# Residual rows added by accumulating DMAs in the second MLP product

## The chip, the cores and the metric

The kernel runs on one core of one Trainium2 chip. A core has TensorE (matrix products, PE in the profile), VectorE (DVE), ScalarE (ACT), GpSimd (POOL) and SyncE (SP), each with a queue of its own that is worked off in order, and 16 DMA engines that move data between HBM, which all queues share, and the core's own memory SBUF. TensorE writes its results to PSUM, in banks of 128 x 512 float32. The metric is the device time of one execution in microseconds, lower is better; of several runs the median is given.

## What is computed

A transformer block on a sequence of 2048 tokens with 1024 channels, in float32: attention with a compressive memory, then an MLP with 3584 hidden channels, each with a residual connection. What matters here is the last part:

```python
h = x + attention(layernorm(x))
y = layernorm(layernorm(h))
h2 = h + gelu(y @ w1 + b1) @ w2 + b2
```

The change concerns the last line: the product of the hidden activations with `w2` (2048 x 3584 times 3584 x 1024), and how `h + b2` is added to it.

## The kernel before

**Precision.** A float32 product is made of three faster ones: both operands are split into a high and a low part (`h`, `l`), and high x high, high x low and low x high are added up in a PSUM bank.

**Stages.** Each half of the sequence goes through attention, the output projection and the first MLP product. After each output projection the rows `h + b2` are written to HBM (`h1_dram`, one tensor of 128 x 1024 for each of the 16 row blocks), and the hidden activations go to `h_dram`. When both halves are through, class `Second` makes the product with `w2` over all 2048 tokens.

**The second product.** It uses a Strassen-like scheme with seven products in place of eight: tokens and channels are each cut in two, and sums and differences of blocks are multiplied. The seven are named "1", "7", "6", "5", "3", "2", "4". For each half of the hidden channels (`s` = 0, 1), each product and each of 8 pairs of row blocks (`p`) there is one job of 21 matmuls: 112 jobs. In the first half, jobs 0 to 15 are products "1" and "7", jobs 16 to 31 "6" and "5", jobs 32 to 47 "3" and "2", jobs 48 to 55 "4"; jobs 56 to 111 repeat this for the second half. Products "7" and "5" go on in the bank of "1" and "6" of the same pair, after the adds of those have read it.

**Output tiles.** The 2048 x 1024 result stands as 32 tiles `c` of 128 x 512 in SBUF (16 row blocks, two column halves), placed by `HOMES` in the order of first use. In `add` (L1427) VectorE adds a finished bank to one or two of them, as `ADDS` says; every tile gets from four to six adds. A tile starts with the residual rows: `out` (L1370) makes the tile and loads its part of `h1_dram` through SP, and `ahead` (L1385) calls it for the tiles of the next two jobs. Each tile is first used in jobs 0 to 15, so the loads fall there. After its last add a tile goes out through SP.

**What feeds a job.** The stationary operands come from the activations: `load_items` loads them through SP into six buffers `hr`; `sums` (L1334 to L1345) adds and subtracts them on GpSimd, two additions for each "6" item, of which there is one for two jobs; `prep` splits the result into the high part (ScalarE, L1360) and the low part (VectorE, L1361), into three buffers taken in turn, two jobs ahead. The moving operands are rows of `w2`: `load_rows` loads them (SP, L1267), `presum` combines two of them on GpSimd where the product needs it (L1278), `fill` splits them (L1286, L1287).

**Order.** The method `work(n, got)` (L1393) writes out what belongs to job `n`, right behind its matmuls: loads, sums, `prep(n + 2)`, the adds of job `n`, fills, more sums, loads, stores, and at the end `ahead(n)`. The whole stage stands in `in_order()`, which ties every instruction to the one before it on its engine in program order. So each queue keeps exactly this order, DMA issues among them, and a waiting instruction holds up all behind it on its engine.

Names of groups in the profile: `c` are the output tiles, `po` the banks, `hr` the activation buffers, `zh`, `zl`, `hl` the three buffers of split operands (and `zh`, `zl`, `w2h`, `w2l` the split rows of `w2`), `w2r` the raw rows. `h_dram` stands for `h1_dram` as well, `s_dram` and `t_dram` for the stored sums of activations and of rows.

Of the kernel before, what the change touches and what calls it, by code (L numbers as in the profile page):

```python
# [13 lines left out]
ALU = mybir.AluOpType  # L14
# [34 lines left out]


def build(tc, x, wq, wk, wv, wo, beta, w1, b1, w2, b2, out):
    nc = tc.nc
    top = ExitStack()
# [38 lines left out]
    h1_dram = [dram.tile([P, D], F32, name=f"h1_dram{t}") for t in range(S // P)]  # L92
# [95 lines left out]
    def interleave(main, side, ratio=1.0, head=0, slow=None):  # L188
        acc = 0.0
        for n, _ in enumerate(main):  # L190
            acc += ratio if slow is None or n < head else slow
            while acc >= 1.0:
                acc -= 1.0
                next(side, None)
        for _ in side:
            pass
# [7 lines left out]
    def chain(*gens):  # L204
        for g in gens:
            yield from g
# [723 lines left out]
    def residual(half, sl, hts, pp):  # L930

        b2c = acts["b2"]

        def aside(t):
            hb = pp.tile([P, D], F32, name="hb", bufs=2)
            nc.vector.tensor_tensor(hb, hts[t], b2c, op=ALU.add)
            nc.sync.dma_start(h1_dram[half * NT + 4 * sl + t], hb)

        return aside
# [75 lines left out]
    HP = FB // 2  # L1015
# [12 lines left out]
    class Mixer:  # L1028
# [6 lines left out]
        def __init__(self, half, mq):  # L1035
            self.half, self.mq = half, mq
            self.p1, self.u, self.ops, self.raw, self.src, self.banks = {}, {}, {}, {}, {}, {}

        def out(self, f, sl, src, tile_=None):
            ht = tile_ if tile_ is not None else self.mq.tile([P, 512], F32, tag="ht", name="ht", bufs=4)  # L1040
            nc.scalar.activation(ht, src, AF.Gelu_apprx_tanh, bias=b1c[:, f:f + 1], scale=1.0)
            t0 = self.half * NT + 4 * sl
            queue = nc.sync if (self.half, f, sl) == (1, HP - 1, 1) else nc.scalar
            queue.dma_start(h_dram[f // 14][f % 14 // 7][t0:t0 + 4, :, f % 7, :].rearrange("t p n -> p t n"),
                            ht.rearrange("p (t n) -> p t n", t=4))
# [146 lines left out]
    class Second:  # L1192
# [16 lines left out]
        def __init__(self, mq):  # L1209
            self.mq = mq  # L1210
            self.jobs, self.items = [], []
            for s in range(2):
                for g in self.GROUPS:
                    n0 = len(self.jobs)
                    seq = [(g[0], 0)]
                    for p in range(self.PAIRS):
                        if len(g) == 1:
                            seq += [(g[0], p + 1)] if p + 1 < self.PAIRS else []
                        else:
                            seq += ([(g[0], p + 1)] if p + 1 < self.PAIRS else []) + [(g[1], p)]  # L1220
                    self.jobs += [(s, n, p) for n, p in seq]
                    for p in range(self.PAIRS):
                        self.items.append((n0 + seq.index((g[0], p)), s, g[0], p))
            first, last = {}, {}
            for n, (s, name, p) in enumerate(self.jobs):
                q = 7 * s + self.SEQ.index(name)
                first.setdefault(q, n)
                last[q] = n
            self.fills = []
            for q in range(14):  # L1230
                lo = last[q - 3] + 1 if q >= 3 else (-8, -8, 2)[q]
                hi = first[q] - 2 if q > 1 else -8
                if hi - lo > self.KP:
                    hi -= 2
                lo = max(lo, hi - 10)
                for k in range(self.KP):
                    self.fills.append((lo + k * (hi - lo + 1) // self.KP, q, k))
            self.fills.sort()
            self.nf = self.nq = self.nl = self.ni = self.ns = 0
            self.slots, self.rows, self.raws, self.srcs, self.hl, self.ps, self.done = {}, {}, {}, {}, {}, {}, []  # L1240
            self.free = list(range(6))
            self.part, self.later = [], []
            self.c, self.np, self.came = {}, 0, {}


        def slot(self, q):
# [123 lines left out]
        def out(self, t, c):  # L1370
            if (t, c) not in self.c:
                pool, tag, bufs = self.HOMES[len(self.c)]
                pool = self.mq if pool == "mq" else acts[pool]
                self.c[t, c] = pool.tile([P, 512], F32, tag=tag, name="c", bufs=bufs)
                nc.sync.dma_start(self.c[t, c], h1_dram[t][:, c * 512:(c + 1) * 512])
            return self.c[t, c]

        NEED = {"1": ("11", "12"), "7": ("21", "22")}
# [3 lines left out]
        def at(self, p, w):  # L1382
            return p + self.PAIRS * (int(w[0]) - 1), int(w[1]) - 1

        def ahead(self, n):  # L1385

            for m in (n + 1, n + 2):
                if m < len(self.jobs) and self.jobs[m][0] == 0:
                    _, name, p = self.jobs[m]
                    for w in self.NEED.get(name, ()):  # L1390
                        self.out(*self.at(p, w))

        def work(self, n, got):  # L1393

            late, self.later = self.later, []
            self.rows_ahead(n)
            self.load_items(n)
            self.sums(n, n + 2)
            self.prep(n + 2)
            self.add(*got)  # L1400
            self.fill_up(n)
            self.sums(n, n + 4)
            self.rows_ahead(n)
            for d, t in late:
                nc.sync.dma_start(d, t)
            self.ahead(n)

        def product(self, n):
            s, name, p = self.jobs[n]
# [17 lines left out]
        def add(self, s, name, p, ps):  # L1427
            for w in self.ADDS[name]:
                t, c = self.at(p, w)
                o = self.out(t, c)  # L1430
                nc.vector.tensor_tensor(o, o, ps, op=ALU.subtract if name == "4" else ALU.add)  # L1431
                if s == 1 and w in self.LAST.get(name, ""):
                    self.later.append((out[0, t * P:(t + 1) * P, c * 512:(c + 1) * 512], o))

# [13 lines left out]
    for half in range(2):  # L1448
# [34 lines left out]
        second = wo_second(half, hts1, ready)  # L1483
# [34 lines left out]
        if half == 0:  # L1518
            for j in range(HP - 9):
                for _ in mixer.pair(j):  # L1520
                    pass
            acts["ahead"] = ln1(1, 1, gap=2)
            interleave(chain(*(mixer.pair(j) for j in range(HP - 9, HP))),
                       chain(ln1(1, 0, 2, tags=("qk",)), islice(acts["ahead"], 3)), 0.17)
            mp.release()
            mq.release()
            zx.release()
            zt.release()
        else:
            second = Second(mq)  # L1530
            fill_at = [(j, 5) for j in range(HP - 8, HP - 2)] + [(HP - 3, 13), (HP - 2, 12), (HP - 2, 15), (HP - 2, 18),
                       (HP - 1, 4), (HP - 1, 8), (HP - 1, 12)]
            for j in range(HP):
                if j == HP - 1:
                    mp.release()
                    acts["sp"] = sp = tc.alloc_tile_pool(name="sp", bufs=1, side="right", reuse_waits="tile")
                for n, _ in enumerate(mixer.pair(j)):
                    if (j, n) == (HP - 9, 8):
                        second.rows_ahead(-10)
                    if (j, n) == (HP - 1, 0):  # L1540
                        second.load_items(-2)
                    if (j, n) in fill_at:
                        second.fill_up(-8, 1)
                        second.rows_ahead(-10)
                    if (j, n) == (HP - 1, 1):
                        second.presum(second.nl)
                    if (j, n) in ((HP - 1, 8), (HP - 1, 9)):
                        second.prep(n - 8, "gpsimd")
                    if (j, n) == (HP - 1, 9):
                        second.sums(0, 2)  # L1550
                    if (j, n) == (HP - 1, 12):
                        second.ahead(-1)
            second.prep(2)
            wp.release()
            acts["cl"] = cl = tc.alloc_tile_pool(name="cl", bufs=1, reuse_waits="tile")
            cl.tile([P, 512], F32, tag="r", name="c", bufs=4)
            cl.tile([P, 512], F32, tag="w", name="c", bufs=12)
            acts["cx"] = cx = tc.alloc_tile_pool(name="cx", bufs=1, reuse_waits="tile")
            second.run()
# [25 lines left out]
```

## Time and profile before

| | |
|---|---|
| median of 3 runs | 2171.73 us (2170.75 to 2175.35) |
| the profiled execution | 2171.36 us |
| its span in the profile | 2169.3 us |
| DMA queue of SP | 289306 packets, 337.25 MB |
| DMA queue of ScalarE | 62928 packets, 36.84 MB |
| DMA queue of GpSimd | none |
| HBM | 241.27 MB read, 82.38 MB written |

The profile is one execution. Times in its views count from the start of the span. Busy time of an engine leaves out register, branch, semaphore and DMA-issuing instructions. In a list in order of time the columns are start, length, engine, line, operation, output <- inputs, shape, and in brackets the time that the engine stood idle just before and what ended that. Matmul lengths overlap: they are issued closer together than one takes.

### The profile page before, as it was taken

The page shows a single profiled execution, that of the slowest core. Times are in us where ns is not written, and L with a number is a line of the kernel's source. Part 1 is how long each engine was busy: PE and PEld are TensorE (multiplying, and loading weights), DVE is VectorE, ACT ScalarE, POOL GpSimd, SP SyncE. Part 2 cuts the span into 40 slices and gives each one's busy share as a digit, 9 for nine tenths or more (in the row PEclk, how much of TensorE's full clock was granted, in tenths as well). Part 3 has the DMA queues.
Part 4 walks back from the last instruction along what each step waited for, and adds up shares of the span by engine and source line. Part 5 has one row for each costly group of instructions (what it writes and reads, how often), then busy time and mean ns, then how long its engine had stood idle before and what let it go on. Part 6 is the DMA issues. An engine that isn't in the chain of part 4 may idle for free.

```text
span 2169.3 us, 33213 instructions
## 1 busy us (share of the span) xinstructions
PE 2150.5 (99%) x10937; PEld 1747.6 (81%) x10937; DVE 1352.7 (62%) x2696; ACT 1099.4 (51%) x2433; POOL 957.8 (44%) x1210
## 2 busy tenths in 40 slices
PE   7999999999999999999999999999999999999999
PEld 6877777778888888877777778888888888888887
DVE  7766666655745666766667655745666665577653
ACT  5777777752543445777777753633343232322221
POOL 5633335561434435533335551534446544256340
PEclk9999999999999999999999999999999999999999
DMA  7444445664575555544445663666569875676762
GB/s 202 128 107 107 108 108 137 192 203 153 170 213 155 179 164 152 130 109 108 106 109 136 195 220 125 185 201 174 159 210 375 278 224 179 203 242 230 252 220 90
DMA packets 352405, 376.20 MB, mean 173 GB/s; under 512 B 27214, under 2 KB 244330, under 8 KB 352234
## 3 DMA queue, kind: packets, MB, share of 16 engines
q1 hardware_dynamic: 289306, 337.25, 51.3%
q10 hardware_dynamic: 62928, 36.84, 5.7%
q8 instruction: 87, 1.43, 0.3%
q14 instruction: 84, 0.69, 0.1%
HBM read 241.27 MB, written 82.38 MB: 149 GB/s over the span
## 4 chain that ended last, share of the span: by engine, by line
PE 92%; DVE 3%; ACT 2%; DMA 2%; POOL 1%; issue 1%; ACTq 0%; SPq 0%; POOLq 0%; DVEq 0%
PE po L1421 22%; PE bps L1024 10%; PE cps L1024 7%; PE dps L1024 6%; PE pst L622 4%; PE po L636 3%; PE pqk L572 3%; PE vps L126 3%; PE pwo L126 3%; PE kps L126 3%; PE vps L127 3%; PE pwo L127 3%; PE pwo L128 3%; PE vps L128 3%; PE qps L126 3%; PE qps L127 2%
## 5 line engine op out<-in xcount | busy, mean ns | idle before, releaser
L574 DVE CUSTOM_DVE_ANT_0 pqk<-pqk,mask 128x512 f32<-128x512 f32 (+2 forms) x384 | 216.9, 565 | 238.1 <-PE pqk L572 211.4
L576 ACT ACTIVATE junk<-pqk,mx 128x512 f32<-128x512 f32 (+2 forms) x384 | 225.1, 586 | 130.4 <-DVE mx L574 124.1
L629 POOL TENSOR_SCALAR_AFFINE_SELECT e<-e 128x128 f32<-128x128 f32 (+1 forms) x384 | 137.0, 359 | 258.7 <-ACT e L625 253.1
L703 POOL TENSOR_TENSOR wl<-wr,wh 128x256 fp32r<-128x256 f32 x268 | 201.1, 766 | 103.8 <-PE pqk L572 89.6
L625 ACT ACTIVATE e<-pst 128x384 f32<-128x384 f32 (+1 forms) x384 | 200.8, 529 | 64.9 <-PE pst L622 62.8
L1431 DVE TENSOR_TENSOR c<-c,po 128x512 f32<-128x512 f32 x160 | 105.6, 683 | 152.8 <-PE po L1421 145.9
L622 PE MATMUL pst<-qs,ks 128*128 128x512 f32 (+3 forms) x512 | 139.5, 315 | 1.7 <-ACT e L625 0.5
L572 PE MATMUL pqk<-ks,qs 96*128 96x512 f32 (+2 forms) x384 | 137.0, 357 | 0.8 <-ACT junk L576 0.6
L622 PEld LDWEIGHTS pst<-qs,ks 128*128 128x128 f32 x512 | 95.3, 188 | 34.6 <-ACT e L625 10.3
L1421 PE MATMUL po<-w2h,zh 128*128 128x512 f32 x378 | 121.0, 390 | 0.7 <-DVE zh L1361 0.4
L1278 POOL TENSOR_TENSOR w2r<-w2r 128x512 f32<-128x512 f32 x54 | 86.1, 1605 | 71.3 <-DMA w2r<-in_B_w 41.3
L126 PE MATMUL kps<-yh,wh 128*128 128x512 f32 (+1 forms) x264 | 112.9, 428 | 0.0
L126 PE MATMUL qps<-yh,wh 128*128 128x512 f32 x256 | 112.8, 441 | 0.0
L1024 PE MATMUL bps<-zh,sb 128*128 128x512 f32 x336 | 111.0, 391 | 0.0
L1024 PE MATMUL bps<-zh,sa 128*128 128x512 f32 x336 | 110.8, 390 | 0.0
L1137 POOL TENSOR_TENSOR s<-r 128x512 f32<-128x512 f32 x28 | 44.0, 1570 | 141.8 <-DVE sa L1153 85.2
L126 PE MATMUL vps<-yh,wh 128*128 128x512 f32 x256 | 104.9, 410 | 0.0
L127 PE MATMUL kps<-yl,wh 128*128 128x512 f32 (+1 forms) x264 | 102.5, 388 | 1.0 <-DVE yl L289 0.6
L1421 PE MATMUL po<-w2h,hl 128*128 128x512 f32 x322 | 103.1, 390 | 0.2 <-DVE hl L1361 0.2
L128 PE MATMUL kps<-yh,wl 128*128 128x512 f32 (+1 forms) x264 | 101.6, 385 | 0.0
L127 PE MATMUL vps<-yl,wh 128*128 128x512 f32 x256 | 100.8, 394 | 0.0
L128 PE MATMUL qps<-yh,wl 128*128 128x512 f32 x256 | 100.5, 393 | 0.0
(272 smaller groups left out, 6202.2 us busy)
## 6 DMA issues: line engine op xcount, KB each, us to landing
hr<-h_dram SPq DMA_DIRECT2D x112, 448.0 KB, 5.1
w2r<-in_B_w SPq DMA_DIRECT2D x122, 256.0 KB, 4.6
r<-in_B_w SPq DMA_DIRECT2D x56, 512.0 KB, 4.2
ks<-kk SPq DMA_DIRECT2D x360, 64.0 KB, 2.0
qs<-qq SPq DMA_DIRECT2D x360, 64.0 KB, 2.0
h_dram<-ht ACTq DMA_DIRECT2D x83, 256.0 KB, 3.7
wx<-in_B_w SPq DMA_DIRECT2D x56, 256.0 KB, 3.5
o_dram<-side SPq DMA_DIRECT2D x52, 256.0 KB, 4.2
```

What stands on the lines that cost most here:

```text
L126: nc.tensor.matmul(ps, ah, bh, start=first, stop=False)
L127: nc.tensor.matmul(ps, ah, bl, start=False, stop=False)
L128: acts["mm"] = nc.tensor.matmul(ps, al, bh, start=False, stop=last)
L572: nc.tensor.matmul(ps, u["qs"][0:96, j, i * P:(i + 1) * P], u["ks"][0:96, j, 0:n], start=True, stop=True)
L574: nc.vector.tensor_tensor_reduce(out=ps, in0=ps, in1=mask[:, 512 - n:512], op0=ALU.add, op1=ALU.min, scale=-SCALE, scalar=3.0e38, accum_out=m)
L576: at(now[0] + 1, lambda: nc.scalar.activation(acts["junk"][:, :n], ps, AF.Exp, bias=m, scale=-1.0, accum_out=u["mx"][:, 1, i, j:j + 1]))
L622: nc.tensor.matmul(ps[:, o:o + 512 - P * jk], u["ks"][:, j, jk * P:(jk + 1) * P], u["qs"][:, j, jk * P:512], start=True, stop=True)
L625: nc.scalar.activation(e, ps[:, :w], AF.Exp, scale=SCALE)
L629: nc.gpsimd.affine_select(d, d, pattern=[[0, 2], [1, P]] if n == 2 else [[1, P]], compare_op=ALU.is_ge, fill=0.0, base=0, channel_multipli ...
L703: nc.gpsimd.tensor_tensor(l[:, c], wr[:, c], raw(h)[:, c], op=ALU.subtract)
L1024: nc.tensor.matmul(ps, x_[:, c, :], y_[:, c, :], start=first and c == 0 and n == 0, stop=last and c == 3 and n == 2, skip_group_check=True)
L1421: nc.tensor.matmul(ps, x_[:, k], y_[k], start=opens and k == 0 and i == 0, stop=closes and k == self.KP - 1 and i == 2, skip_group_check=True)
```

## The change

An output tile no longer begins with the residual rows. The first product that reaches a tile is copied into it, later ones are added as before. The residual rows are added on the way by a DMA that accumulates into the tile, issued by GpSimd. `plan` gives each tile a job, from job 20 on, one tile a job: after the tile's first use, and such that no add of the tile falls in that job or the three behind it. All 32 fit into jobs 20 to 51. The next add of the tile is over 30 jobs away for the DMAs of jobs 20, 21, 23 and 25, and exactly 4 jobs away for the others. `residual(n)` stands where `ahead(n)` stood, at the end of `work(n)`; the early call of `ahead`, from the last pair of the first product, goes too.

```diff
@@ __init__
             self.c, self.np, self.came = {}, 0, {}
+            self.plan()
@@ out
                 self.c[t, c] = pool.tile([P, 512], F32, tag=tag, name="c", bufs=bufs)
-                nc.sync.dma_start(self.c[t, c], h1_dram[t][:, c * 512:(c + 1) * 512])
             return self.c[t, c]
@@
-        def ahead(self, n):
-
-            for m in (n + 1, n + 2):
-                if m < len(self.jobs) and self.jobs[m][0] == 0:
-                    _, name, p = self.jobs[m]
-                    for w in self.NEED.get(name, ()):
-                        self.out(*self.at(p, w))
+        LATE = 20
+
+        def plan(self):
+
+            uses = {}
+            for n, (s, name, p) in enumerate(self.jobs):
+                for w in self.ADDS[name]:
+                    uses.setdefault(self.at(p, w), []).append(n)
+            self.rest, left, n = {}, sorted(uses, key=lambda k: uses[k][-1]), self.LATE
+            while left:
+                k = next((k for k in left if uses[k][0] < n and not any(n <= m < n + 4 for m in uses[k])), None)
+                if k:
+                    assert uses[k][-1] > n
+                    self.rest[n] = k
+                    left.remove(k)
+                n += 1
+
+        def residual(self, n):
+
+            if n in self.rest:
+                t, c = self.rest[n]
+                nc.gpsimd.dma_start(self.c[t, c], h1_dram[t][:, c * 512:(c + 1) * 512], accum_op=ALU.add)
@@ work
-            self.ahead(n)
+            self.residual(n)
@@ add
+                bare = (t, c) not in self.c
                 o = self.out(t, c)
-                nc.vector.tensor_tensor(o, o, ps, op=ALU.subtract if name == "4" else ALU.add)
+                if bare:
+                    nc.vector.tensor_copy(o, ps)
+                else:
+                    nc.vector.tensor_tensor(o, o, ps, op=ALU.subtract if name == "4" else ALU.add)
@@ the loop over the last pairs of the first product
-                    if (j, n) == (HP - 1, 12):
-                        second.ahead(-1)
```

## The prediction

> **What bounds the kernel now.** I read the head of the page first, then the chain that ended last, then the table of stretches for the second MLP product alone.
>
> ```profile
> span 2169.3 us, 33213 instructions
> PE 2150.5 (99%) x10937; PEld 1747.6 (81%) x10937; DVE 1352.7 (62%) x2696; ACT 1099.4 (51%) x2433; POOL 957.8 (44%) x1210
> ...
> PE 92%; DVE 3%; ACT 2%; DMA 2%; POOL 1%; issue 1%; ACTq 0%; SPq 0%; POOLq 0%; DVEq 0%
> ```
>
> TensorE holds the end. The stretches below are jobs 0 to 15 of the second product, jobs 16 to 19, jobs 20 to 31, jobs 32 to 52, and the rest; columns are the length, then busy time by engine, the granted clock, the busy share of the 16 DMA engines and GB/s.
>
> ```profile
> core 0: us, PE busy (x) PEld busy (x) DVE busy (x) ACT busy (x) POOL busy (x), PEclk, DMA share, GB/s
> 1629.00:1706.00 77.00, 76.57 (x337) 62.80 (x336) 50.31 (x57) 23.78 (x31) 48.30 (x25) 1.00 0.96 351
> 1706.00:1724.00 18.00, 17.28 (x76) 13.65 (x75) 13.35 (x15) 5.64 (x8) 10.08 (x7) 1.00 0.82 262
> 1724.00:1784.00 60.00, 60.00 (x266) 49.59 (x265) 35.26 (x43) 16.97 (x23) 29.36 (x13) 1.00 0.69 226
> 1784.00:1886.00 102.00, 102.00 (x451) 84.46 (x451) 60.22 (x67) 31.10 (x42) 28.64 (x16) 1.00 0.56 184
> 1886.00:2166.00 280.00, 279.34 (x1231) 230.59 (x1230) 164.76 (x178) 73.59 (x95) 115.88 (x56) 1.00 0.64 211
> ```
>
> The reader is to see two things. The whole stage leaves TensorE idle for 0.43 + 0.72 + 0 + 0 + 0.66 = 1.8 us out of 537, so nothing done here can win more than about that, 0.08%. And the DMA engines are full (0.96) in the stretch where the change takes loads away, and have room (0.69, 0.56) where it puts new ones. A measurement of this kernel can tell about 0.2%, 4.3 us, from no change.
>
> **What goes: 32 loads on SP.** The loads of residual rows are 32 issues, and their removal can only help TensorE where TensorE waits. The chain of waits around the first jobs names one of them:
>
> ```profile
> 1633.14 5.80 DMA c<-h_dram
> 1638.94 0.02 issue
> 1638.96 0.70 DVE c L1431
> 1639.66 0.14 issue
> 1639.80 20.42 PE po L1421 x89
> ```
>
> Job 2 accumulates into job 0's bank, so it has to wait until both of job 0's adds have read it, and those adds wait for the load that lands at 1638.94. That looks like a stall that goes. But one has to ask what is late next. VectorE in order of time (start, length, engine, line):
>
> ```profile
> 1636.29 2.03 DVE L1361 TENSOR_TENSOR zl<-hr,zl 128x896 fp32r<-128x896 f32 x1 [2.39 <-ACT zl L1360]
> 1638.24 1.41 DVE L1431 TENSOR_TENSOR c<-c,po 128x512 f32<-128x512 f32 x2
> ...
> 1641.77 1.27 DVE L1431 TENSOR_TENSOR c<-c,po 128x512 f32<-128x512 f32 x2
> ```
>
> The lower half of job 2 stands ahead of the pair of adds in VectorE's fixed order and ends at 1638.32. Without the load the pair starts no earlier than now, and runs 1.27 instead of 1.41 us. The gain is 0.14 us; I count **-0.1**. Its bounds are 0 and the 0.43 us that TensorE idles in that stretch. The other idle time, 0.72 us at jobs 16 to 19, comes after the last of these loads has landed (the last is issued at 1696.0 and the slowest landing is 7.9, rows below), so I leave it. SP is spared 32 issues and the DMA engines 32 x 256 KB of the 27 MB that 351 GB/s makes in 77 us, but TensorE is busy there already: worth nothing.
>
> ```profile
> L1375 SPq DMA_DIRECT2D c<-h_dram x32: 319/320/1059, 1631.8 to 1696.0; - x32
> ...
> DMA to landing us min/median/max: 5.5/6.1/7.9
> ```
>
> **What is exchanged: 32 adds for 32 copies.** A copy of one bank to SBUF on VectorE stands in the attention stage, an add in jobs 20 to 52 in the grouped lines:
>
> ```profile
> L459 DVE COPY pkf<-pkn x24: 679/692/692, 33.4 to 1186.3; 128x512 f32<-128x512 f32 x24
> ```
>
> ```profile
> L1431 DVE TENSOR_TENSOR c<-c,po 128x512 f32<-128x512 f32 x43 | 28.8, 684 | 44.9 <-PE po L1421 44.9
> L1361 DVE TENSOR_TENSOR zh<-hr,zh 128x896 fp32r<-128x896 f32 x11 | 15.8, 1434 | 5.2 <-ACT zh L1360 5.2
> L1287 DVE TENSOR_TENSOR w2l<-w2r,w2h 128x512 fp32r<-128x512 f32 x18 | 15.5, 879 | 0.7 <-ACT w2h L1286 0.5
> ```
>
> 692 against 684 ns, 32 times, is 0.3 us of VectorE, which has 77 - 50.31 us free there: nothing.
>
> **What comes: 32 accumulating DMAs in GpSimd's queue.** By the diff's plan there is one for every job from 20 to 51, last in its job's work, so in GpSimd's fixed order two of them stand between the sums of one "6" item and the next: sums of 23, then DMAs 20 and 21, sums of 25, DMAs 22 and 23, sums of 27, DMAs 24 and 25, sums of 29, DMAs 26 and 27, sum of 32. GpSimd now, with its idle time and what ended it:
>
> ```profile
> 1734.30 2.12 POOL L1339 TENSOR_TENSOR hr<-hr 128x896 f32<-128x896 f32 x1 [5.83 <-DMA hr<-h_dram]
> 1736.49 2.12 POOL L1340 TENSOR_TENSOR hr<-hr 128x896 f32<-128x896 f32 x1
> 1744.02 2.66 POOL L1339 TENSOR_TENSOR hr<-hr 128x896 f32<-128x896 f32 x1 [5.41 <-DMA hr<-h_dram]
> 1746.75 2.12 POOL L1340 TENSOR_TENSOR hr<-hr 128x896 f32<-128x896 f32 x1
> 1751.04 2.12 POOL L1339 TENSOR_TENSOR hr<-hr 128x896 f32<-128x896 f32 x1 [2.16 <-DVE zh L1361]
> 1753.64 2.45 POOL L1340 TENSOR_TENSOR hr<-hr 128x896 f32<-128x896 f32 x1 [0.48 <-DMA hr<-h_dram]
> 1759.94 2.43 POOL L1339 TENSOR_TENSOR hr<-hr 128x896 f32<-128x896 f32 x1 [3.85 <-DMA hr<-h_dram]
> 1762.45 2.12 POOL L1340 TENSOR_TENSOR hr<-hr 128x896 f32<-128x896 f32 x1
> 1771.66 2.59 POOL L1345 TENSOR_TENSOR hr<-hr 128x896 f32<-128x896 f32 x1 [7.09 <-DMA hr<-h_dram]
> ```
>
> These are the sums of items 23, 25, 27, 29 and 32. The gaps into which two issues must fit are 5.41, 2.16, 3.85 and 7.09 us. How much TensorE feels is the distance from the end of a job's lower half on VectorE (three rows) to the third matmul of that job, the first that reads it (three rows of TensorE):
>
> ```profile
> 1749.89 1.09 DVE L1361 TENSOR_TENSOR zh<-hr,zh 128x896 fp32r<-128x896 f32 x1 [5.18 <-ACT zh L1360]
> ...
> 1757.09 1.09 DVE L1361 TENSOR_TENSOR hl<-hr,hl 128x896 fp32r<-128x896 f32 x1 [0.45 <-ACT hl L1360]
> ...
> 1765.57 1.09 DVE L1361 TENSOR_TENSOR zl<-hr,zl 128x896 fp32r<-128x896 f32 x1 [3.83 <-ACT zl L1360]
> ```
>
> ```profile
> 1751.16 0.63 PE L1421 MATMUL po<-w2h,zh 128*128 128x512 f32 x2
> ...
> 1760.71 0.62 PE L1421 MATMUL po<-w2h,hl 128*128 128x512 f32 x2
> ...
> 1770.23 0.62 PE L1421 MATMUL po<-w2h,zl 128*128 128x512 f32 x2
> ```
>
> Job 25: 1751.16 - 1750.98 = 0.18 us. Job 27: 2.53. Job 29: 3.57. So **job 25 is the place**: any delay of its sums over 0.18 us stops TensorE.
>
> The time x that GpSimd spends on one such DMA stands in no row. From below, SP issues a DMA of this shape in 0.32 us (above); from above, 2.66 us, GpSimd's longest instruction in these rows. I take 1.3, between the two, nearer to the short one, since an issue moves no data through the engine. Two make 2.6 and fit into 5.41; into 2.16 they don't by 0.44, which job 27's 2.53 covers. The Trainium skill ("DMA: Bandwidth & Descriptors", Latency and other measured facts) puts the first byte of a DMA issued by GpSimd at about 1 us; by that the sum is the same.
>
> The transfers are the second cost. DMAs 20 and 21 would leave from 1738.6 on, while the three loads for item 25 are under way and land at 1744.0. Two times 256 KB at the 351 GB/s of the full stretch are 1.5 us. If all of it goes ahead of the loads' last bytes, they land 1.5 us later; if the destination's read counts as much again, 3.0; if none does, 0. I take 1.2, since the second DMA starts late. Job 25 then stops TensorE for 1.2 - 0.18 = **+1.0**. The stop gives jobs 27 and 29 the same microsecond, so they lose nothing more.
>
> Added waits: each DMA waits for its tile's last add. The tightest is DMA 25 behind job 24's adds, and it is free before GpSimd gets there (1756.09, the end of item 27's sums). The next add of a tile waits for the landing. DMA 22 leaves at 1748.87 + 2.6 = 1751.5 at the latest, and job 26's add uses its tile at 1760.46, 9.0 us later:
>
> ```profile
> 1754.03 1.27 DVE L1431 TENSOR_TENSOR c<-c,po 128x512 f32<-128x512 f32 x2
> ...
> 1760.46 1.28 DVE L1431 TENSOR_TENSOR c<-c,po 128x512 f32<-128x512 f32 x2
> ```
>
> A plain load of these rows lands in 6.1. If this one took twice that, 12.2, VectorE would wait 3.2 us, with job 29's lower half queued behind, which has 3.57: nothing again.
>
> **Sum.** The profiled execution took 2171.36 us, 2.06 outside its span and 0.4 below the median of 2171.73. 2171.36 - 0.1 + 1.0 = **2172.3**.
>
> **Rivals.**
> *Hidden entirely* (0.2). The new transfers share the engines after item 25's loads. For it: 0.69 busy. Against it: 0.18 us of cover. 2171.36 - 0.1 = 2171.3.
> *GpSimd's issue is long* (0.1; slower). The gaps give the delay of item 29: 1.2 + (2x - 2.16) + (2x - 3.85), less its 3.57. It passes 4.4 us, and so 0.2%, from x = 3.2 us; at x = 4 the first gap gives way too (2.59 in place of 1.2) and the sum is 9.0: 2180.3. At the row's bound, 2.66, it is 2.3: 2173.6. For it: a GpSimd add already takes 2.12 or 2.66 us, by what runs beside it. The Trainium skill ("SBUF — State Buffer", SBUF: two separate sides, the trap of a VectorE operation that blocks a GpSimd DMA) says that a VectorE copy from SBUF to SBUF holds the port through which GpSimd writes its descriptors. By that rule x would be stretched by VectorE; but VectorE runs only TENSOR_TENSOR in jobs 20 to 52 (the grouped lines above; the ones not shown are the same three lines), and the new copies read PSUM and are over by job 15, so the trace gives it a small chance.
> *The DMA engines become the bound in jobs 20 to 31* (0.07; slower). A plain transfer takes 256 KB / (226 / 0.69 GB/s) = 0.8 us of all 16; 0.31 x 60 us are free for 13 of them, 1.43 each. From 1.8 times the plain price on, loads fall behind; at three times, 13 x (2.4 - 1.43) - 3.57 = 9 us: 2180.
> *More is won than I see* (0.03). All 1.8 us go: 2169.6, no measurable difference either; over 4.3 us I see no place for, and leave 0.02 to it.
> That the change does not do what it says I see no room for: each DMA's place is fixed by the order on GpSimd.
>
> The forecast has 0.6. Faster 0.02; slower 0.1 + 0.07 = 0.17, rounded with the forecast's own tail to 0.18; the same 0.80. The range is 2169.6 (all idle time gone) to 2176.5: past x = 2.66 and the doubled transfer (2171.36 + 2.8 = 2174.2), leaving out the worse part of the two slower cases.
>
> **What would show it.** Right: no c load on SP, no stop before job 2's copies other than the 0.1; GpSimd's DMA issues about 1.3 us; a stop of about 1 us before job 25's third matmul and none at 27 to 31. Wrong: GpSimd idle-free from 1738 to 1770, a stop at job 27 or 29, VectorE waiting on an accumulating DMA, or a DMA share near 1.0 in jobs 20 to 31.

## The result and the profile after

| | before | after |
|---|---|---|
| median | 2172.03 us (2170.67 to 2176.58) | 2184.15 us (2182.13 to 2185.29) |
| ratio | | 1.0054, 95% interval [1.0045, 1.0064] |
| the profiled execution, its span | 2171.36, 2169.3 us | 2184.85, 2182.8 us |

The change costs about 12 us. The head of the page, the sum of the chain that ended last, and the queues (packets, MB, share of 16 engines over the span) of the kernel after:

```profile
PE 2154.1 (99%) x10937; PEld 1748.7 (80%) x10937; DVE 1363.9 (62%) x2696; ACT 1099.4 (50%) x2433; POOL 979.8 (45%) x1242
...
q1 hardware_dynamic: 284698, 328.86, 50.1%
...
q0 software_dynamic: 4608, 8.39, 2.4%
...
PE 89%; DMA 3%; DVE 3%; ACT 1%; POOL 1%; issue 1%; SPq 0%; ACTq 0%; POOLq 0%; DVEq 0%
```

The row of q0 is the first number that was missing before: 2.4% of 2182.8 us in 32 transfers is **1.64 us of all 16 engines for each accumulating DMA**. The stretches of the second product, as in the prediction:

```profile
1629.00:1706.00 77.00, 77.00 (x341) 63.63 (x340) 57.02 (x59) 24.03 (x32) 50.13 (x25) 1.00 0.74 244
1706.00:1724.00 18.00, 17.39 (x76) 13.76 (x75) 11.65 (x12) 5.01 (x7) 11.83 (x6) 1.00 0.86 297
1724.00:1784.00 60.00, 60.00 (x266) 49.36 (x265) 34.02 (x41) 15.40 (x21) 29.77 (x20) 1.00 0.85 238
1784.00:1886.00 102.00, 94.38 (x409) 77.36 (x407) 65.47 (x63) 30.02 (x40) 47.95 (x39) 0.97 0.86 226
1886.00:2166.00 280.00, 277.40 (x1218) 227.93 (x1217) 166.53 (x183) 75.95 (x99) 114.38 (x58) 1.00 0.66 219
```

Jobs 20 to 31 show no idle time at all; the DMA share there went from 0.69 to 0.85. The time is lost behind them, in the stretch from 1784 (102 - 94.38 = 7.6 us, with a lower clock) and in the last (2.6). TensorE in order of time finds the place, the first three matmuls of job 37 (the last of them is the first that reads the lower half of the split operand):

```profile
1809.59 0.50 PE L1436 MATMUL po<-zh,zh 128*128 128x512 f32 x1 [1.65 <-ACT zh L1361]
1809.93 0.40 PE L1436 MATMUL po<-zl,zh 128*128 128x512 f32 x1
1816.29 1.22 PE L1436 MATMUL po<-zh,zh 128*128 128x512 f32 x2 [5.97 <-DVE zh L1362]
```

The operand of job 37 is late: its upper half by 1.65 us, its lower half by another 5.97. The granted clock (the last column but two) fell during this stop and stayed low behind it, 0.50 from 1812.8 to 1819.6:

```profile
1809.50:1816.30 6.80, 0.74 (x3) 0.31 (x3) 6.80 (x3) 3.05 (x5) 5.78 (x5) 0.75 0.61 94
1816.30:1822.20 5.90, 5.90 (x19) 4.77 (x20) 3.74 (x5) 0.00 (x0) 1.60 (x1) 0.72 0.90 245
1822.20:1829.00 6.80, 6.80 (x32) 5.63 (x31) 5.65 (x5) 2.52 (x3) 5.45 (x5) 1.00 0.96 270
```

The second row has 19 matmul records in 5.90 us, the third 32 in 6.80. One starts every 0.227 us otherwise, 26 in 5.90 us: the seven that are missing are 1.6 us more. So job 37 costs 1.65 + 5.97 + 1.6 = 9.2 us of idle and slow time; by the starts of the matmuls, from job 36 to job 38, it is 9.8 of the 12.7 us by which the stage grew. 2.4 more stand at jobs 55 to 57 and 1.7 at jobs 80 and 81, and elsewhere it is 1.2 less, 0.9 of that in jobs 0 to 2.

Why is the operand late? GpSimd's sums in order of time, after: the first sum of each of the items 25, 29, 32, 33, 35 and 37 (an item has the number of the first job that uses it):

```profile
1741.98 2.11 POOL L1340 TENSOR_TENSOR hr<-hr 128x896 f32<-128x896 f32 x1 [3.40 <-DMA hr<-h_dram]
...
1763.55 2.12 POOL L1340 TENSOR_TENSOR hr<-hr 128x896 f32<-128x896 f32 x1 [6.05 <-DMA hr<-h_dram]
...
1778.30 2.11 POOL L1346 TENSOR_TENSOR hr<-hr 128x896 f32<-128x896 f32 x1 [8.69 <-DMA hr<-h_dram]
...
1784.33 2.56 POOL L1346 TENSOR_TENSOR hr<-hr 128x896 f32<-128x896 f32 x1 [3.08 <-DMA hr<-h_dram]
...
1789.35 2.12 POOL L1346 TENSOR_TENSOR hr<-hr 128x896 f32<-128x896 f32 x1 [0.72 <-DMA hr<-h_dram]
...
1803.78 2.11 POOL L1346 TENSOR_TENSOR hr<-hr 128x896 f32<-128x896 f32 x1 [10.42 <-DMA hr<-h_dram]
```

The same sums of items 33, 35 and 37 before, and VectorE's lower half of job 37 and TensorE's third matmul of it:

```profile
1777.60 2.12 POOL L1345 TENSOR_TENSOR hr<-hr 128x896 f32<-128x896 f32 x1 [3.35 <-DMA hr<-h_dram]
1780.08 2.12 POOL L1345 TENSOR_TENSOR hr<-hr 128x896 f32<-128x896 f32 x1 [0.36 <-DMA hr<-h_dram]
1795.01 2.82 POOL L1345 TENSOR_TENSOR hr<-hr 128x896 f32<-128x896 f32 x1 [12.81 <-DMA hr<-h_dram]
```

```profile
1800.81 3.01 DVE L1361 TENSOR_TENSOR zh<-hr,zh 128x896 fp32r<-128x896 f32 x1
```

```profile
1808.32 0.62 PE L1421 MATMUL po<-zh,zh 128*128 128x512 f32 x2
```

The lag, after against before, is -2.0 us at item 25 (1741.98 - 1744.02: the loop has run ahead), about 0 at 27 (1750.97 against 1751.04), then +3.6 at 29, +6.6, +6.7, +9.3, +8.8 at 37. Every row is released by a load. Job 37 had 1808.32 - 1803.82 = 4.5 us in hand; a lag of 8.8 is past that. The loads themselves, by the DMA view of the stretch 1724 to 1810 (columns: size, median us from issue to landing), before and then after:

```profile
hr<-h_dram SPq DMA_DIRECT2D x18, 448.0 KB, 5.7
w2r<-in_B_w SPq DMA_DIRECT2D x17, 256.0 KB, 5.4
hr<-s_dram SPq DMA_DIRECT2D x7, 448.0 KB, 4.9
s_dram<-hr SPq DMA_DIRECT2D x5, 448.0 KB, 7.1
w2r<-t_dram SPq DMA_DIRECT2D x6, 256.0 KB, 4.1
```

```profile
hr<-h_dram SPq DMA_DIRECT2D x17, 448.0 KB, 6.4
w2r<-in_B_w SPq DMA_DIRECT2D x15, 256.0 KB, 7.8
c<-h_dram POOLq DMA_DIRECT2D x15, 256.0 KB, 7.9
hr<-s_dram SPq DMA_DIRECT2D x6, 448.0 KB, 7.2
s_dram<-hr SPq DMA_DIRECT2D x5, 448.0 KB, 9.2
w2r<-t_dram SPq DMA_DIRECT2D x4, 256.0 KB, 7.7
```

Each of these loads and stores takes 0.7 to 3.6 us longer, and in the loop each step waits for the one before (load, sum, store, load into the buffer that comes free). One turn's delay is small enough to be covered; the lag is carried on from turn to turn until the cover is gone.

The last step, from the late sum to the still later lower half, is on VectorE:

```profile
1808.73 4.35 DVE L1288 TENSOR_TENSOR w2l<-w2r,w2h 128x512 fp32r<-128x512 f32 x1 [9.59 <-ACT w2h L1287]
1813.01 3.23 DVE L1362 TENSOR_TENSOR zh<-hr,zh 128x896 fp32r<-128x896 f32 x1
```

The sum is 8.8 late, the lower half 1816.24 - 1803.82 = 12.4. It stands behind a split of W2 rows that waited 9.59 us and then took 4.35.

### The profile page after: what moved, and what is told of

Its sections match the earlier page's. It is cut to its first block, busy times and chain, and to the rows that moved or that the text cites. A ratio compares the mean times of both kernels' runs of the same rounds, so it can differ in the third digit from the quotient of the medians.

```text
span 2182.8 us, 33232 instructions
## 1 busy us (share of the span) xinstructions
PE 2154.1 (99%) x10937; PEld 1748.7 (80%) x10937; DVE 1363.9 (62%) x2696; ACT 1099.4 (50%) x2433; POOL 979.8 (45%) x1242
## 3 DMA queue, kind: packets, MB, share of 16 engines
q0 software_dynamic: 4608, 8.39, 2.4%
q8 instruction: 87, 1.43, 0.3%
## 4 chain that ended last, share of the span: by engine, by line
PE 89%; DMA 3%; DVE 3%; ACT 1%; POOL 1%; issue 1%; SPq 0%; ACTq 0%; POOLq 0%; DVEq 0%
PE po L1436 18%; PE bps L1024 10%; PE cps L1024 7%; PE dps L1024 7%; PE pst L622 4%; PE po L636 3%; PE pqk L572 3%; PE vps L126 3%; PE pwo L126 3%; PE kps L126 3%; PE vps L127 3%; PE pwo L127 3%; PE pwo L128 3%; PE vps L128 3%; PE qps L126 3%; PE qps L127 2%
## 5 line engine op out<-in xcount | busy, mean ns | idle before, releaser
L1450 DVE TENSOR_TENSOR c<-c,po 128x512 f32<-128x512 f32 x128 | 84.8, 683 | 105.8 <-PE po L1436 105.5
```

## Experiments

Theories: **A**, the time that an accumulating transfer holds the 16 DMA engines delays the loop's loads; **B**, GpSimd's issue and its place in the queue; **C**, any 8.4 MB moved into these jobs. All times in one table; "before" is measured beside each group, on the same chip, so compare ratios and not medians of different groups. The ratio is the recorded estimate, not the quotient of the two medians. There are 10 or 11 runs of each kernel, of e5, e12 and e14 only 4 or 5.

| kernel | median us | before | ratio [95%] |
|---|---|---|---|
| e1_none | 2172.12 | 2172.34 | 0.9995 [0.9985, 1.0004] |
| e2_plain_gp | 2172.55 | 2172.34 | 1.0004 [0.9994, 1.0013] |
| e3_plain_sp | 2172.84 | 2172.34 | 1.0001 [0.9992, 1.0011] |
| e4_small_acc | 2170.86 | 2172.34 | 0.9996 [0.9987, 1.0005] |
| e5_twice_plain | 2186.10 | 2172.95 | 1.0060 [1.0046, 1.0074] |
| e6_half_acc | 2174.18 | 2172.95 | 1.0009 [0.9999, 1.0018] |
| e7_spread | 2176.81 | 2172.95 | 1.0021 [1.0012, 1.0030] |
| e9_presum_dve | 2177.40 | 2172.95 | 1.0021 [1.0012, 1.0030] |
| e10_slots | 2177.31 | 2173.39 | 1.0017 [1.0008, 1.0026] |
| e11_late38 | 2176.41 | 2173.39 | 1.0017 [1.0007, 1.0026] |
| e12_first16 | 2182.03 | 2173.39 | 1.0037 [1.0024, 1.0050] |
| e13_last16 | 2174.84 | 2173.39 | 1.0008 [0.9999, 1.0017] |
| e14_slots2 | 2180.21 | 2172.17 | 1.0035 [1.0021, 1.0049] |
| e15_slots_no64 | 2173.17 | 2172.17 | 1.0005 [0.9996, 1.0015] |
| e16_before_presum | 2172.61 | 2172.17 | 1.0002 [0.9993, 1.0011] |
| e17_slots3 | 2174.69 | 2172.32 | 1.0008 [0.9999, 1.0017] |

**Which property of the 32 DMAs costs.** Four edits, each alone (e2, e3 and e4 replace the same line of `residual`):

```diff
 e1_none
-            self.residual(n)
 e2_plain_gp
-nc.gpsimd.dma_start(self.c[t, c], ..., accum_op=ALU.add)
+nc.gpsimd.dma_start(self.c[t, c], ...)
 e3_plain_sp
+nc.sync.dma_start(self.c[t, c], ...)
 e4_small_acc
+nc.gpsimd.dma_start(self.c[t, c][:, 0:16], h1_dram[t][:, c * 512:c * 512 + 16], accum_op=ALU.add)
```

> The changed kernel without its 32 accumulating DMAs: the residual is left out of the result; copies at first touch stay. All theories: what is left is the gain of removing the 32 loads, about 2171 us (2170 to 2172), stop of job 2 gone, no stop at job 37, DMA share in jobs 20 to 31 about 0.6. If the time stays above 2178, the loss comes from the copies or from the lost pacing of the first jobs, and all theories that blame the accumulating DMAs fall.

> The same 32 DMAs at the same places, issued by GpSimd, without accumulation: they overwrite the output tile, so part of the sum is lost. Theory A (the accumulating transfer holds the DMA engines 1.9 times as long as a plain one): a plain transfer takes about half, 0.9 us of 16 engines against 1.64, and the time falls to 2174 or less. Theory B (GpSimd's queue: issue time and its place between the sums): 2182 to 2186, as with accumulation. Theory C (any 8.4 MB of transfers moved from the first jobs to jobs 20 to 51 do it): 2182 to 2186.

> The same 32 DMAs at the same places in the program, issued by SyncE, without accumulation: they overwrite the output tile. Theory A: 2174 or less. Theory B: about 2171, since GpSimd issues nothing any more. Theory C: 2182 to 2186. If it is slower than 2186, SyncE's in-order queue, in which each of these DMAs waits for the tile's last add, is a price of its own.

> The same 32 accumulating DMAs at the same places on GpSimd, with 16 of their 512 columns: the rest of the residual is left out. The issue and the place in GpSimd's queue stay, most of the traffic goes. Theory A: about 2171 to 2173. Theory B: 2182 to 2186. Theory C: about 2171 to 2173.

All four are as fast as before. Issue and queue place stay in e4 (the grouped line of GpSimd: count, busy us, mean ns), so B falls. Bytes and places stay in e2 and e3, so C falls:

```profile
L1406 POOL DMA_DIRECT2D c<-h_dram x32 | 31.7, 1139 | 1.1 <-issue 1.0
```

What differs is the queue's row, here of e2:

```profile
q0 software_dynamic: 2560, 8.39, 1.1%
```

1.1% of 2171.6 us in 32 is 0.75 us for a plain transfer; with accumulation 1.64, 2.2 times as much, for the same 8.39 MB. In the trace the plain one's packets carry 4096 bytes, two rows; the accumulating one's carry 2048, and there are 4608 of them instead of 2560.

**Is it the engines' time, or accumulation as such?** Two plain transfers in place of one accumulating, and an accumulation of half the width:

```diff
 e5_twice_plain
+x_dram = [dram.tile([P, 512], F32, name=f"x_dram{t}") for t in range(32)]
 ...
-nc.gpsimd.dma_start(self.c[t, c], ..., accum_op=ALU.add)
+nc.gpsimd.dma_start(self.c[t, c], ...)
+nc.gpsimd.dma_start(x_dram[n - 20], h1_dram[t][:, c * 512:(c + 1) * 512])
 e6_half_acc
+nc.gpsimd.dma_start(self.c[t, c][:, 0:256], h1_dram[t][:, c * 512:c * 512 + 256], accum_op=ALU.add)
```

> At each of the 32 places GpSimd issues two plain transfers in place of the accumulating one: the residual rows over the output tile (which loses part of the sum), and the same rows once more into an unused DRAM tile. Two plain ones hold the 16 DMA engines about 1.5 to 1.7 us, as one accumulating one does (1.64 us), and GpSimd issues for about 1.1 us, as before (1.05 us). Theory A1 (it is the time on the DMA engines, whatever the transfer is for): 2178 to 2186, with the load-sum-store loop some 5 to 10 us late at the sum of item 37. Theory A2 (something else in an accumulation, such as its reading of the tile or the order of its packets): 2171 to 2174.

> The same 32 accumulating DMAs with 256 of their 512 columns: the other half of the residual is left out. Each should hold the 16 engines about 0.85 to 1.0 us, near a plain full transfer. Theory A1: 2171 to 2174, as the plain full one (2172.6). Theory A2: about half of the loss of 12 us, 2177 to 2179. If the loss has a threshold between the two sizes, A1 and A2 agree here and the double plain transfer decides.

Their queue rows, e5 first:

```profile
q0 software_dynamic: 5120, 16.78, 2.3%
```

```profile
q0 software_dynamic: 4608, 4.20, 1.3%
```

Engine time at each place: 0.75 us (e2), 0.88 (e6), 1.57 (e5, both together), 1.64 (after). Loss against before: 0, 1.2 (not told from 0), 13 and 12 us. Without any accumulation, e5 loses as much as the change, and at the same place: its sum of item 37 begins at 1804.82, and TensorE waits 1.1 and 4.8 us for the operand of job 37. Bytes, packets and issue don't order the four like this: e2 moves as many bytes as the change, e6 as many packets, and GpSimd spends 1.1 us on e5's two issues but 1.14 on the one of e4, which cost nothing. So **the time on the DMA engines decides**, with a steep rise between 0.88 and 1.57. In e2 and e6 that sum is 5.0 and 5.6 us late already (1799.96 and 1800.59 against 1795.01), and the lower half of job 37 ends less than 0.1 us before its third matmul: there the cover is just used up. The stretches of jobs 20 to 23, 24 to 27, 28 to 31 and 32 to 35 in e1_none (DMA share in the last column but one) say where it should lie:

```profile
1724.80:1743.90 19.10, 19.10 (x86) 15.83 (x85) 12.71 (x17) 5.13 (x7) 6.74 (x3) 1.00 0.73 231
1743.90:1763.00 19.10, 19.10 (x85) 15.60 (x84) 11.43 (x12) 4.61 (x6) 11.25 (x6) 1.00 0.64 212
1763.00:1782.00 19.00, 19.00 (x85) 15.73 (x84) 11.40 (x12) 7.22 (x10) 8.11 (x4) 1.00 0.67 225
1782.00:1801.10 19.10, 19.10 (x86) 15.80 (x85) 12.89 (x18) 6.44 (x9) 6.17 (x5) 1.00 0.78 272
```

Free: 5.2 + 6.9 + 6.3 + 4.2 = 22.5 us for 16 transfers, 1.4 each, by that estimate. The 16 x 1.64 = 26.2 us asked for are 3.7 too many; the lag at item 37 is 8.8, and the same four stretches are 0.79, 0.95, 0.81 and 1.03 busy after the change. This suggests that a loop that waits for landings can't use all of the free time.

**Where the loss is made.** The first 16 of the 32 alone, and the last 16 alone:

```diff
 e12_first16
-            if n in self.rest:
+            if n in self.rest and n < 36:
 e13_last16
+            if n in self.rest and n >= 36:
```

> Only the first 16 accumulating DMAs, those of jobs 20 to 35; those of jobs 36 to 51 are left out with their half of the residual. Theory A with a lag carried on from turn to turn of the load-sum-store loop: the sum of item 37 is as late as with all 32 (8 to 9 us), a stop of 4 to 10 us at job 37, 2177 to 2183. If the stop is made beside job 37 by DMAs and sums there: no stop, 2171 to 2173.

> Only the last 16 accumulating DMAs, those of jobs 36 to 51; those of jobs 20 to 35 are left out with their half of the residual. Theory A with a lag carried on: the sum of item 37 in time within 1 us, no stop at job 37; what is left of the loss is that of jobs 55 to 81, at most 4 us: 2171 to 2175. If the stop is made beside job 37: 2177 to 2183.

The first 16 keep 8.6 of the 12 us. The sum of item 37 is late, and so is the operand of job 37 (GpSimd, then TensorE of e12):

```profile
1805.89 2.12 POOL L1346 TENSOR_TENSOR hr<-hr 128x896 f32<-128x896 f32 x1 [10.05 <-DMA hr<-h_dram]
```

```profile
1817.49 0.80 PE L1436 MATMUL po<-zh,zh 128*128 128x512 f32 x1 [5.06 <-DVE zh L1362]
```

With the last 16 alone that sum is in time, 1795.19 against 1795.01, and there is no stop (GpSimd of e13):

```profile
1795.19 2.12 POOL L1346 TENSOR_TENSOR hr<-hr 128x896 f32<-128x896 f32 x1 [12.91 <-DVE c L1450]
```

The lag is made by the accumulations of jobs 20 to 35 and paid at job 37.

**The last step, from the sum to the lower half.** GpSimd's row sums for the blocks beside job 37 are moved to VectorE, in the changed kernel (e9) and, as a control, in the kernel before (e16):

```diff
-nc.gpsimd.tensor_tensor(x0, x0, x1, op=...)
+(nc.vector if q == 6 else nc.gpsimd).tensor_tensor(x0, x0, x1, op=...)
```

> The changed kernel as it is, with the 7 sums of rows for the seventh set of W2 blocks (those which stand beside job 37) made by VectorE instead of GpSimd. Theory D (the stop at job 37 is made long by GpSimd's and VectorE's sums of two SBUF tiles blocking each other: 4.35 us for a sum that takes 0.69 us, then 3.23 us for the lower half of job 37, 1.08 us otherwise): the stop falls by 4 to 6 us, the time to 2176 to 2181. If only the late loads make it: 2182 to 2185, the stop as long as before.

> The kernel before the change, with the seven sums of W2 rows beside job 37 made by VectorE instead of GpSimd (as in e9_presum_dve): a control. If the gain of e9 is the shortening of the changed kernel's stop at job 37, nothing changes here, 2171 to 2174. If that edit is worth some us in itself: 2164 to 2169, and e9 says nothing of the stop.

The sum of item 37 is as late as ever, but the lower half is not; GpSimd, then VectorE of e9:

```profile
1803.97 2.11 POOL L1346 TENSOR_TENSOR hr<-hr 128x896 f32<-128x896 f32 x1 [10.71 <-DMA w2r<-in_B_w]
```

```profile
1801.41 0.69 DVE L1288 TENSOR_TENSOR w2l<-w2r,w2h 128x512 fp32r<-128x512 f32 x1 [0.69 <-ACT w2h L1287]
...
1807.08 1.09 DVE L1362 TENSOR_TENSOR zh<-hr,zh 128x896 fp32r<-128x896 f32 x1 [4.98 <-ACT zh L1361]
```

The split of W2 rows now runs at 1801.41 in 0.69 us instead of 1808.73 in 4.35, the lower half in 1.09 instead of 3.23, and the stop at job 37 is gone; the loss falls from 12 to 4.5 us. The control is as fast as the kernel before, so by itself the edit is worth nothing that can be told. In e9 the lower half ends at 1808.17, 4.35 us later than before and just inside the 4.5 in hand: the stop needs both, the late sum and the work that stands beside it at job 37. Of what is left of the loss, 2.9 us stand at jobs 54 to 57, by the starts of their matmuls. Two things went together and were not taken apart: the row sum no longer stands behind the late sum in GpSimd's queue, and VectorE no longer runs beside GpSimd's sums. The Trainium skill ("SBUF — State Buffer", Who interferes with whom) says that a VectorE operation with two SBUF inputs contends with a GpSimd instruction that reads SBUF; 4.35 us for a 0.69 us operation agrees with that. My expectation called 1.08 us the usual length of this lower half; beside GpSimd's sums it took 3.01 before, too.

**Other places for the accumulations.** Six plans; e15 is e10 without eight of the accumulations, the others add the whole residual. With SLOTS the plan goes through the listed jobs, in place of every job from LATE on:

```diff
 e7_spread
-                n += 1
+                n += 2
 e11_late38
-        LATE = 20
+        LATE = 38
 e10_slots
+        SLOTS = sorted([*range(38, 50), *range(44, 48), *range(64, 72), *range(96, 104)])
 e15_slots_no64
+            if not 64 <= n < 72:
+                self.residual(n)
 e14_slots2
+        SLOTS = sorted([*range(38, 52), *range(40, 50), *range(96, 104)])
 e17_slots3
+        SLOTS = sorted([*range(7, 15), *range(38, 50), *range(44, 48), *range(96, 104)])
```

> All 32 accumulating DMAs, full size, at every second job from 20 on instead of at every job: the whole residual is added. Theory A (DMA engines over-asked in jobs 20 to 37): the extra share falls from 1.64/4.77 = 0.34 to 0.17, near that of plain transfers at every job (0.75/4.77 = 0.16), so 2171 to 2174. A theory that each accumulation costs by itself, wherever it stands (12.4 us / 32 = 0.39 us each): 2182 to 2186.

> The changed kernel with the accumulations at jobs 38 to 69, one each, instead of 20 to 51; the whole residual is added. Theory A: no stop at job 37, but jobs 56 to 59 have a DMA share of 0.91 without them, and the extra 0.34 passes 1: stops in jobs 55 to 65, time 2176 to 2184. A theory that only GpSimd's dense stretch at job 37 matters: 2171 to 2173.

> All 32 accumulating DMAs, full size, the whole residual added, but at jobs where the profile without them (e1_none) shows the DMA engines least busy: 38 to 49 one each, 44 to 47 a second one, 64 to 71 and 96 to 103 one each. The DMA share there is 0.54, 0.43, 0.24, 0.70 (four jobs each from 36), 0.66, 0.48 (from 64) and 0.49 (from 96); one accumulation a job adds 0.34. Theory A (time on the DMA engines, while they have little to spare): 2171 to 2173.5, no stop over 1 us at job 37. A theory that every accumulation costs 0.39 us wherever it stands: 2182 to 2186.

> The kernel of e10_slots without its eight accumulations at jobs 64 to 71; their part of the residual is left out. Theory A: the stop at job 75 (5 us with them) falls below 1 us and the time to 2171 to 2174. If the 16 at jobs 38 to 49 or the 8 at 96 to 103 make the loss: 2176 to 2178, the stop unchanged.

> All 32 accumulating DMAs, full size, the whole residual added: one each at jobs 38 to 51, a second one at 40 to 49, one each at 96 to 103; none ahead of jobs 72 to 75. Theory A with a lag that is paid where the loop has no slack (job 75, whose lower half ends 0.1 us ahead of its third matmul already before): 2171 to 2174, no stop over 1 us at job 75; two a job (0.69 of the 16 engines) on 0.43 and 0.24 just fit. A theory that accumulations cost wherever they stand: 2177 or more.

> All 32 accumulating DMAs, full size, the whole residual added: the 24 of e15_slots_no64 where they were, and the eight of jobs 64 to 71 at jobs 7 to 14 instead, where the kernel before the change had a DMA share of 1.04 with no stop. Theory A (an accumulation costs only where the loop of loads and sums has no slack left): 2171 to 2174, no stop over 1 us at jobs 19, 37, 55 or 75. If 32 full accumulations cannot be had for nothing anywhere: 2176 or more.

e11 came as expected: job 37 is clear, and TensorE waits 3.3 us for a lower half at job 56 (its profile is of the slowest of its runs, 2180.98; the runs of e7, e10 and e11 spread over 7 to 10 us). e7 and e10 lie 3 and 4 us above what I expected, e14 6. In each the stop moved to the next place with little in hand behind the accumulations: jobs 75 and 85 in e7, 75 in e10, 54 and 55 in e14. The waits of TensorE from 1950 to 2000 in e10, and from 1880 to 1910 in e14 (total us, times, longest):

```profile
PE po L1434 <- ACT hl L1361: 2.0, 1, 2.0
```

```profile
PE po L1434 <- ACT zh L1361: 3.0, 1, 3.0
```

e15 points to e10's cause: without the eight at jobs 64 to 71 TensorE waits for nothing from 1950 to 2000, and the loss against before falls from 3.9 to 1.0 us, though the intervals of the two still overlap; the other 24 accumulations cost nothing that can be told. So no price shows that an accumulation would have wherever it stands; but the mean DMA share of a stretch, by which I had put the slots, doesn't show how much lag the loop can carry into the next tight job. e17 puts those eight at jobs 7 to 14: 1.0008, not told from no change, though 0.7 us above what I expected, and its profile has stops of 1.5 and 0.4 us at job 19, where the kernel before has 0.3 and 0.4. No version beat the kernel before. The fastest, e4 at 2170.86, leaves nearly all of the residual out and is not told from it either.

## Why the prediction failed, step by step

The forecast was 2172.3 us, a stop of 1.0 at job 25; measured were 2184.15, with the loss at job 37 and behind. The step that failed is the transfers: their price, and how far their delay reaches.

- **What bounds the stage: right.** At most 1.8 us could be won; e1_none, with the loads gone and nothing in their place, is not told from before.
- **The copies, and no wait on a landing: right.** No copy and no wait of VectorE for an accumulating DMA stands in the losses.
- **GpSimd's issue, 1.3 us: right in kind, a little high.** The 32 issues have a median of 0.89 us (0.86 to 1.81), and e4 shows that they are covered:

```profile
L1406 POOL DMA_DIRECT2D c<-h_dram x32: 860/890/1807, 1736.6 to 1892.7; - x32
```

- **The gain of 0.1 at job 2: not to be told.** By the starts of their matmuls jobs 0 to 2 take 15.3 us before and 14.4 after, 0.9 less, which is past the bound of 0.43 that counted idle time alone. But e16, which still has the 32 loads, takes 14.4 there too, and e12, which has none of them, 16.3: from one profile to the next these jobs vary by more than the term.
- **The stop of 1.0 at job 25: did not come.** The sum of item 25 ran 2.0 us ahead, and the 0.18 us of cover on which the +1.0 rested was 2.1 us. Why stays open: in e1_none, with neither the loads nor the accumulations, it is 0.06.
- **The transfers: the step that failed, in two of its terms.** First the price: I took 1.5 us for two transfers, 0.75 each, and 1.2 as their effect. 0.75 is what a plain one takes; the accumulating one takes 1.64. Second, and worse, the reach: "the stop gives jobs 27 and 29 the same microsecond, so they lose nothing more" followed one turn of the loop and stopped at job 31, while the DMAs go on to job 51. The lag adds up over six turns (-2.0 to +8.8 us) and shows where it passes the cover, at job 37, which the prediction never looked at.
- **The rival "the DMA engines become the bound": right, and given 0.07.** Its plain price (0.8) and its point (1.43 us) hold: 0.88 costs about nothing and 1.57 the whole. Its time, 2180, needed three times the plain price; at the measured 2.2 times its formula gives 13 x (1.64 - 1.43) = 2.7 us, less than job 29's 3.57 of cover, so no loss. It was short by jobs 32 to 35, where the share is 0.78, and by what GpSimd's and VectorE's order adds at job 37 (3.6 us between the late sum and the lower half).
- **The halved clock** was in no step: 1.6 us behind the stop at job 37. The Trainium skill ("TensorE: Matmul & The Clock Gate", Why this matters for your kernels) warns of idle gaps of over about 3 us; the stop of 5.97 us agrees, with 0.75 granted over the 6.80 us around it and 0.72 over the 5.90 behind.
- Of the signs named as wrong, a stop at job 27 or 29 is there at 29 only, with 0.3 us by the starts of the matmuls (its 3.57 us of cover were down to 0.06), and a share of 0.85 is not quite "near 1.0"; the place to look was behind these jobs.

## What to carry to other kernels

Where DMAs are put beside a loop of loads, sums and stores, add up the engines' time that they ask for against what the loop leaves free, over the whole stretch in which they are issued, and follow the lag from turn to turn to the first job with little in hand, not to the first one after the change. Price an accumulating DMA apart from a plain one of the same bytes. A mean share (0.69 here) doesn't say how much time the engines can give beside a chain in which each load waits for the one before: 0.88 us a job cost nothing that can be told, 1.57 cost 13.

## What the runs showed of the hardware

- A DMA from DRAM that accumulates 128 x 512 float32 into SBUF held the 16 engines for 1.64 us, a plain one issued by the same engine 0.75. At half the width it still took 0.88, with as many packets (4608).
- GpSimd was busy 0.89 us (median) with the issue of an accumulating DMA, 1.05 on average; of 16 columns alone, 1.11 and 1.14, so it doesn't go by bytes.
- Eight accumulations ahead of job 75 (e10 against e15) moved the loss from 1.0 to 3.9 us; the 24 others by themselves cost nothing that can be told.
